# A fused attention and snake-activation kernel: the opening's order of work, and the last output rows in two column parts

## The chip, the cores and the metric

The kernel runs on one core of a Trainium2 chip. A core has a matrix engine (TensorE, PE in the profile, with its weight loads listed apart as PEld), VectorE (DVE), ScalarE (ACT), GpSimd (POOL) and SyncE (SP), which only issues DMAs here. POOL and ACT issue DMAs too. Each engine takes its own instructions strictly in the order in which the program gives them; semaphores tie the engines together, so an instruction that waits holds up all that stands behind it on its engine.

The metric is the device time of one execution in microseconds, lower is better. Three runs of the kernel before gave 377.85, 378.79 and 378.56 us, so the median is 378.56 us.

## The reference, cut to what matters

```python
# q, k, v: (8, 8, 576, 64); bias_table: (32, 8); w_in: (512, 2048); w_out: (2048, 512); alpha: (2048,)
scores = q @ k.T / sqrt(64) + bias_table[bucket(|i - j|)]     # per batch and head
attn   = softmax(scores)
x      = (attn @ v), heads side by side                         # (4608, 512)
h = x @ w_in
g = h + sin(alpha * h) ** 2 / (alpha + 1e-9)
out = g @ w_out                                                 # (4608, 512) float32
```

The bucket of a distance is the distance itself below 16, grows with its logarithm up to 128 and is the last bucket beyond. So the bias differs from a constant only in a band of about 128 keys on each side of the diagonal.

## The kernel before

**Work.** There are eight batches (index t). A batch has eight heads, taken as four pairs (index p), and 576 queries and keys. `plan_unit` makes one unit of attention: a score product on PE (keys on the partitions, a pair of heads side by side), `exp` on ACT out of PSUM, and, for the blocks that touch the band, a multiplication on DVE with `m2r`, which holds exp(bias) relative to the last bucket, row by row shifted. Unit kinds are A (128 keys by 512 queries, two heads), C (the last 64 keys; its band part is `mhr`, multiplied on POOL for pairs 1 to 3 of batch 0 and on DVE otherwise), B and X (the last 64 queries). `plan_av` multiplies the weights with v on PE, divides by the row sum on DVE (`norm_av`, lines 933 to 941), turns the result on PE or by a transposing DMA, and copies it to `xT`. `plan_moe_in` takes 512 rows of x at a time: for each of 16 chunks of `w_in` four matmuls, `Sin` and often `Square` on ACT, the other squares and the combination to `g` on DVE. `plan_mo` makes the output: 16 accumulating matmuls of 512 columns for 128 rows, one copy out of PSUM (`outs`), one DMA of 256 KB from SP. There are nine blocks of 512 output rows; the last block's last rows are the end of the kernel.

**Opening.** Batch 0 does not wait for a staged and transposed copy of q and k. Its pairs are loaded as they are (`nat0` for pair 0 from SP, `nat1` for pairs 1 to 3 from POOL by `load_pair`) and turned on PE (`plan_tr`): k first, then q, each turn copied out of PSUM on DVE to `kT` and `qT`. The small last key block goes to `kt` on POOL (`tail`, line 577). Pair 0 is first cast to 16 bits: k on DVE, q half on ACT (line 514) and half on POOL (line 515).

The band needs a chain of its own: `less_last` times the table on PE (line 509), `exp` on ACT (line 511), a product with a one-hot matrix on PE (line 591), a copy to `e_sb` on ACT (line 594), a DMA of 40 KB to `e_dram` issued by ACT (line 595), and then loads from `e_dram` issued by SP: `m2r` for heads 0 and 1, `mhr` in two DMAs, `m2r` for heads 2 and 3 and for heads 4 to 7 (lines 599 to 602). Behind those SP issues four loads of v for heads 4 to 7 (`load_v32`), which land in the memory of `w_out` and are cast on POOL (`cast_v`).

POOL's queue carries `load_pair`, the loads of v for the last keys (`load_vt`) and for heads 2 and 3 (`load_vh`), the casts of v, the key tails, the C multiplications, the clearing of batch 1's buffers (`clear`), `w_in` in four DMAs (`load_w_in16`, two calls of two), batch 1's q and k and `w_out` (`loads2`) and batch 1's v (`loads3`). Batch 1's q and k are turned on PE as well (`plan_tr` with t = 1), in the middle of the first block's `Sin` work.

PE would otherwise stand idle in the opening; filler matmuls on zeros (`warm`, `warm1`, and `pad` behind some tasks) fill part of it.

**What sets the order.** Apart from a short fixed start (lines 482 to 515), the order on every engine is worked out by a list planner when the program is built (`Plan.run`). Each task has an estimated duration per engine, dependences, a priority (`pri`, lower first) and an earliest time in the planner's own clock (`nb`). The planner always emits the task that can start first, and among those within 0.02 us of each other the one with the lower priority. The constants `T_...` (lines 218 to 241) are such earliest times: for the turns of pair 0 (`T_FIRST`) and of pairs 1 to 3 (`T_PAIR`), the second table product (`T_E`), the v loads and casts (`T_V0`, `T_VA`, `T_VB`), the band multiplications of pairs 0 to 3 (`T_M2`) and of the C units (`T_MH`), `clear` (`T_CL`), `w_in` (`T_WI`), `alpha` (`T_AL`: time and priority), batch 1's turns (`T_TR1`: k, q) and the quarters of `w_out` (`T_WO`). They are the author's picture of when data arrive; a real wait is by semaphore, whatever the planner thought.

Of the kernel before, what the change touches and what calls it, by code (L numbers as in the profile page):

```python
# [20 lines left out]
def t_pe(n):  # L21
    return n / 2400.0 + 0.0025
# [192 lines left out]
T_START = 4.0  # L215
SPLIT = {0: 3, 1: 3}
PRI_S = 0
T_WI = 16.7
T_E = 5.9
T_CL = 20.5  # L220
T_FIRST = (5.2, 6.3)
T_PAIR = ((7.0, 7.4), (8.8, 9.4), (11.0, 11.6))
T_ACT = ()
T_M2 = (13.0, 14.5, 16.0, 16.0)
T_MH = 15.8
T_RST = 25.0
T_V0 = (7.5, 8.2, 8.9, 9.6)
T_VA = (10.5, 11.0)
T_VB = (16.3, 17.8, 18.3, 18.8)
T_AL = (20.0, 100)  # L230
LATE = 100
T_LD = 33.0
AV_LATE = 9000
# [2 lines left out]
NORM0 = 1200  # L236
SQ = {"ACT": 0.52, "DVE": 0.38}
T_V = ((15.5, 19.0), (50.0, 50.0))
T_TR1 = (36.5, 38.0)
T_W = (25.5, 30.5)  # L240
T_WO = (41.0, 43.5, 46.5, 49.5)
WARM0 = 8
WARM1 = 5
WARM_LAG = 0.3
WARM_GAP = 0.12
WARM_FROM = 7.3
# [19 lines left out]
def kernel(  # L266
# [239 lines left out]
    warm(WARM0)  # L506
    for _ in range(WARM1):
        warm1(7, 192)
    full(pb[0:NB, 1, 0:H], less_last, tabN, True, True)
    warm1(7, 192)  # L510
    nc.scalar.activation(out=tabE, in_=pb[0:NB, 1, 0:H], func=AF.Exp)
    cast0(0, nc.vector)
    x0 = nat0[:, 1].rearrange("s two (i d) -> s i two d", i=SI)
    nc.scalar.activation(out=natb[:, 1, :, 0], in_=x0[:, :, 0], func=AF.Copy)
    P_.tensor_copy(out=natb[:, 1, :, 1], in_=x0[:, :, 1])

    def loads2():
# [22 lines left out]
    def plan_tr(t, p, kq, pri, nb, deps=()):  # L540

        b, c = Buf("mo"), Cell()

        def mm(e):
            c.v = bank(b).bitcast(F16)
            for i in range(SI):
                x = i * SN
                if t == 0 and p == 0:
                    nc.tensor.transpose(
                        out=c.v[:, x : x + SN], in_=natb[:, kq, i], identity=id_sb[0:SN, 0:SN]  # L550
                    )
                    continue
                for z in range(2):
                    h = 2 * p - 2 + z if t == 0 else 2 * p + z
                    nc.tensor.transpose(  # L555
                        out=c.v[64 * z : 64 * z + 64, x : x + SN],
                        in_=(nat1 if t == 0 else nat2)[:, kq, h, D * i : D * i + D],
                        identity=id_sb[0:SN, 0:SN],
                    )

        def cp(e):
            pin = c.v[:, 0:S].rearrange("d (i p) -> d p i", i=SI)

            dst = (kTs, qTs)[kq][t][:, p, :]
            copy_on(e, dst.rearrange("d (p i) -> d p i", i=SI), pin)

        m = plan.add({"PE": 0.4 if t == 0 and p == 0 else 0.5}, mm, deps, pri, nb, new=[b])
        if t == 0:
            m.pad = (256,) if p else (192,) * (5 if kq else 1)
        eng = {"DVE": 0.75, "ACT": 0.6}  # L570
        if t == 0:
# [12 lines left out]
        return [x], [plan.add({"POOL": 0.4 if t == 0 else 0.5}, tail, [x], pri + 30)]  # L584

    def plan_table():

        b = Buf("h")

        def mm(e):  # L590
            full(bank(b)[0:H, 0:EW], tabE, phi_sb, True, True)

        def cp(e):
            nc.scalar.activation(out=e_sb, in_=bank(b)[0:H, 0:EW], func=AF.Copy)  # L594
            nc.scalar.dma_start(
                out=e_dram.ap()[:, 0:H].rearrange("r h x -> h r x"),
                in_=e_sb.unsqueeze(1).to_broadcast([H, NE, EW]),
            )
            load_m2r(nc.sync, 0, 2, 0)
            load_mhr(nc.sync)  # L600
            load_m2r(nc.sync, 2, 4, 3)
            load_m2r(nc.sync, 4, H, 4)
            for h in range(4, H):
                load_v32(h)

        x = plan.add({"PE": 0.25}, mm, [], -1100, nb=T_E, new=[b])
        plan.add({"ACT": 1.0}, cp, [x], -1100, use=[b])

    def plan_v0():
        plan.add({"POOL": 1.4}, lambda e: load_pair(3), [], -950, nb=5.8)  # L610
        for i in range(2):
            plan.add({"POOL": 0.45}, lambda e, i=i: cast_v(i), [], 9004 + i, nb=T_VA[i])
# [12 lines left out]

# [317 lines left out]
    def plan_av(t, parts, u, ub, done, base, dma):  # L943
# [154 lines left out]

    def plan_mo(b, a):

        mb, ob, m = Buf("mo"), Buf("outs"), Cell()
        for f in range(NF):

            def mm(e, f=f):
                if f == 0:
                    m.v = bank(mb)
                full(
                    m.v, gcell[b].v[:, f, 128 * a : 128 * a + 128], w_out16[:, f, :],
                    f == 0, f == NF - 1,
                )  # L1110

            mo_last[:] = [plan.add({"PE": t_pe(512)}, mm, mo_last[:] + [gdone[(b, f)]],
                                   500000000 + 4 * b + a, nb=T_WO[f // 4] if b == 0 else 0.0, new=[mb] if f == 0 else [],
                                   use=[gbuf[b]] if f == 0 else [gbuf[b], mb])]
            mo_last[0].fill = True

        def cp(e):
            o = new_outs()
            copy_on(e, o, m.v)
            r0 = 512 * b + 128 * a  # L1120
            nc.sync.dma_start(out=out[r0 : r0 + 128, :], in_=o)

        y = plan.add({"DVE": t_dve(512), "ACT": t_act(512)}, cp, mo_last[:], CP_PRI,
                     new=[ob], use=[mb])
        y.s_only = True

    def set_table(name):
        nc.scalar.preload_act_table_set(name)  # L1128
# [83 lines left out]
```

## Time and profile before

| | us |
|---|---|
| median of 3 runs | 378.56 |
| the profiled execution | 378.73 |
| its span, from the first to the last instruction | 377.0 |
| PE busy | 367.7 |
| ACT busy | 311.8 |
| DVE busy | 260.7 |
| POOL busy | 91.7 |
| mean granted TensorE clock | 0.998 |

The time of an execution has 1.73 us beside the span of its instructions. The page of the profile lists busy times, the span in 40 slices, the DMA queues, the chain of work that ended last, and groups of instructions. The timeline view lists instructions in order of time: start, duration, engine, line and what is written from what, the number of instructions merged in the row, and in brackets how long the engine stood idle before it and who released it. The chain view lists start, duration and what. The view of DMA issues has the number of issues, the size of one and the median time from issue to landing. The view by windows has the busy time of each engine in a stretch.

### The profile page before, as it was taken

How to read it: one execution, taken by the hardware profiler on the slowest of the kernel's cores; microseconds unless marked ns; L12 is line 12 of the kernel's file. 1: busy time of each engine (PE TensorE's matmuls, PEld its weight loads, DVE VectorE, ACT ScalarE, POOL GpSimd, SP SyncE). 2: the span in 40 equal slices, each digit the busy share in tenths (PEclk: the TensorE clock that was granted, in tenths of full speed). 3: DMA queues.
4: the chain of work that ended last, by engine and by line, in shares of the span. 5: the costliest groups of instructions: out<-in, count | busy, mean ns of one | idle time of the engine just before them, and what ended most of it. 6: DMA issues, size and time to landing. Idle time of an engine off the chain costs nothing.

```text
span 377.0 us, 8905 instructions
## 1 busy us (share of the span) xinstructions
PE 367.7 (98%) x3568; PEld 195.7 (52%) x3568; DVE 260.7 (69%) x563; ACT 311.8 (83%) x426; POOL 91.7 (24%) x132
## 2 busy tenths in 40 slices
PE   8889899999999999999999999999999999999995
PEld 4464445644464446864554455445675465444442
DVE  4596867688678867695769676976788677939000
ACT  2988999999898899897979797979897997969111
POOL 7476370064001900091007300550032000000000
PEclk9999999999999999999999999999999999999999
DMA  9989999399627992499349962999299220010212
GB/s 172 149 159 207 200 170 154 71 142 124 101 57 163 85 156 79 84 114 161 87 84 145 141 105 54 148 137 132 57 142 84 62 70 16 0 56 3 83 57 84
DMA packets 148970, 40.49 MB, mean 107 GB/s; under 512 B 137064, under 2 KB 143296, under 8 KB 148928
## 3 DMA queue, kind: packets, MB, share of 16 engines
q0 software_dynamic: 96032, 17.67, 57.9%
q1 hardware_dynamic: 52720, 22.16, 25.1%
q8 instruction: 28, 0.46, 0.5%
q10 hardware_dynamic: 176, 0.09, 0.1%
q14 instruction: 14, 0.11, 0.1%
HBM read 37.73 MB, written 16.56 MB: 144 GB/s over the span
## 4 chain that ended last, share of the span: by engine, by line
PE 87%; DMA 6%; ACT 3%; POOL 2%; SPq 1%; issue 0%; DVE 0%; ACTq 0%
PE pb L453 86%; DMA nat<-in_q_dram 3%; ACT u L692 3%; DMA w_out<-in_v_dram 1%; DMA e_dram<-e_sb 1%; POOL w_in L434 1%; PE pb L555 1%; POOL v L418 0%; SPq L469 0%; PE pb L1009 0%; SPq L476 0%; POOL u L709 0%; POOL nat L428 0%; ACT outs L536 0%; ACT e_sb L594 0%
## 5 line engine op out<-in xcount | busy, mean ns | idle before, releaser
L692 ACT ACTIVATE u<-pb 128x1024 f16<-128x1024 f32 (+1 forms) x146 | 136.0, 1020 | 15.7 <-PE pb L453 15.3
L453 PE MATMUL pb<-w_out,g 128*128 128x512 f16 x576 | 138.3, 380 | 0.0
L453 PE MATMUL pb<-xT,w_in 128*128 128x512 f16 (+4 forms) x704 | 127.9, 340 | 0.0
L1067 DVE SCALAR_TENSOR_TENSOR g<-sq,inv_a,pb 128x512 f16<-128x512 f16 x144 | 101.1, 743 | 10.4 <-PE pb L453 5.6
L1053 ACT ACTIVATE s<-pb,alphaT 128x512 f16<-128x512 f32 x144 | 92.8, 691 | 13.2 <-PE pb L453 12.3
L453 PEld LDWEIGHTS <-w_in 128*128 128x128 f16 x704 | 64.4, 98 | 57.3 <-DMA w_in<-in_moe_w_in_dram 0.4
L453 PEld LDWEIGHTS <-g 128*128 128x128 f16 x576 | 52.6, 98 | 63.4 <-issue 8.5
L723 DVE TENSOR_TENSOR u<-u,m2r 128x512 f16<-128x512 f16 (+1 forms) x128 | 61.9, 494 | 27.5 <-ACT u L692 24.4
L453 PEld LDWEIGHTS <-u 128*128 128x128 f16 x1152 | 44.4, 97 | 9.4 <-issue 2.8
L398 POOL COPY kt<-kT 64x256 f16<-64x256 f16 x12 | 5.1, 427 | 173.4 <-DMA kT<-staged_k 173.1
L453 PE MATMUL pb<-qT,kT 64*128 64x64 f16 (+1 forms) x512 | 44.3, 286 | 0.5 <-ACT u L692 0.2
L453 PE MATMUL pb<-v,u 128*128 128x65 f16 x1024 | 44.5, 193 | 0.2 <-ACT u L692 0.2
L1060 ACT ACTIVATE sq<-s 128x512 f16<-128x512 f16 x66 | 41.5, 637 | 1.2 <-DVE g L1067 0.3
L1062 DVE TENSOR_TENSOR sq<-s 128x512 f16<-128x512 f16 x78 | 32.6, 426 | 14.0 <-ACT s L1053 12.9
L938 DVE TENSOR_TENSOR xn<-pb,rd 128x256 f16<-128x256 f32 (+2 forms) x59 | 28.5, 483 | 2.0
L453 PE MATMUL pb<-vh,u 128*128 128x130 f16 x128 | 28.2, 220 | 0.3 <-DVE xn L938 0.2
L453 PEld LDWEIGHTS <-kT 64*128 64x128 f16 x512 | 16.1, 94 | 23.7 <-issue 16.1
L403 POOL DMA_DIRECT2D v<-in_v_dram x28 | 24.7, 896 | 6.1 <-DMA nat<-in_k_dram 2.3
L536 ACT ACTIVATE outs<-pb 128x512 f32<-128x512 f32 x10 | 6.0, 597 | 23.2 <-PE pb L453 23.2
L937 DVE RECIPROCAL rd<-pb 128x4 f32<-128x4 f32 (+2 forms) x59 | 11.0, 187 | 16.0 <-PE pb L453 15.1
L538 DVE COPY outs<-pb 128x512 f32<-128x512 f32 x26 | 17.9, 687 | 3.6 <-PE pb L453 3.6
L1128 ACT ACT_TABLE_LOAD x15 | 19.2, 1283 | 0.3
(74 smaller groups left out, 188.1 us busy)
## 6 DMA issues: line engine op xcount, KB each, us to landing
out_dram<-outs SPq DMA_DIRECT2D x36, 256.0 KB, 2.3
v<-in_v_dram POOLq DMA_DIRECT2D x28, 128.0 KB, 4.8
staged_k<-in_k_dram POOLq DMA_DIRECT2D x6, 576.0 KB, 8.6
staged_q<-in_q_dram POOLq DMA_DIRECT2D x6, 576.0 KB, 13.0
w_in<-in_moe_w_in_dram POOLq DMA_DIRECT2D x4, 512.0 KB, 8.4
w_out<-in_moe_w_out_dram POOLq DMA_DIRECT2D x4, 512.0 KB, 16.7
w_out<-in_v_dram SPq DMA_DIRECT2D x6, 128.0 KB, 5.4
xT<-xn SPq DMA_TRANSPOSE x47, 2.4
```

Of the source, the lines that this page charges most:

```text
L403: nc.gpsimd.dma_start(out=vs[t % 2][:, c, :, 0:D], in_=vp[128 * c : 128 * c + 128],)
L453: nc.tensor.matmul(out=out, lhsT=lhsT, rhs=rhs, start=start, stop=stop)
L538: k_of(e).tensor_copy(out=o, in_=i)
L692: nc.scalar.activation(out=o, in_=x, func=AF.Exp, scale=0.125)
L723: nc.vector.tensor_tensor(out=io, in0=io, in1=m2[:, 2 * p : 2 * p + 2, x0 : x0 + hi - lo], op=ALU.mult)
L937: nc.vector.reciprocal(out=r, in_=x[:, :, :, D])
L938: nc.vector.tensor_tensor(out=xn[:, 0:n].rearrange("p c (z d) -> p c z d", z=2), in0=x[:, :, :, 0:D], in1=r.unsqueeze(3).to_broadcast([128 ...
L1053: nc.scalar.activation(out=s16.v, in_=h.v, func=AF.Sin, scale=alphaT[:, f : f + 1])
L1060: nc.scalar.activation(out=sq.v, in_=s16.v, func=AF.Square)
L1062: k_of(e).tensor_tensor(out=sq.v, in0=s16.v, in1=s16.v, op=ALU.mult)
L1067: nc.vector.scalar_tensor_tensor(out=gcell[b].v[:, f, :], in0=sq.v, scalar=inv_a[:, f : f + 1], in1=h.v, op0=ALU.mult, op1=ALU.add,)
L1128: nc.scalar.preload_act_table_set(name)
```

## The change

Six things change, nearly all of them places in the order.

1. *Start.* Two filler matmuls of 192 columns instead of five come before the first turn. The first table product leaves the fixed start and becomes a planned task behind the k turn of pair 0, as do its `exp` and the second product, which come before the q turn. The half cast of q that ACT did goes to DVE.
2. *Turns of batch 0.* All of them get other earliest times: pair 0's earlier (4.75 and 5.95 instead of 5.2 and 6.3), those of pairs 1 to 3 later by 0.5 to 1.1.
3. *POOL's loads.* The loads of pair 3's q and k come behind the two `load_vt`.
4. *w_in.* All four DMAs of `w_in` go out at one place, behind a copy of one element of `m2r` (heads 4 to 7) to `tick`, so POOL waits there for the last band rows; the casts of v for heads 4 to 7 come behind them; `clear` is planned later (24.5 instead of 20.5).
5. *alpha* is turned and inverted at planner time 10 instead of 20; the C multiplications may start earlier; batch 1's k turns may come 0.5 earlier and its q turns 1.0 later; the quarters of `w_out` are expected 0.5 to 1.2 earlier; the planner's estimate of batch 0's division shrinks by 0.11 us.
6. *End.* The last 128 output rows are made in two column parts, 384 and 128 columns, each with its own 16 matmuls, copy and DMA.

```diff
-T_WI = 16.7
-T_E = 5.9
-T_CL = 20.5
-T_FIRST = (5.2, 6.3)
-T_PAIR = ((7.0, 7.4), (8.8, 9.4), (11.0, 11.6))
+T_WI = 16.8
+T_TAB = 5.2
+T_CL = 24.5
+T_FIRST = (4.75, 5.95)
+T_PAIR = ((7.9, 8.5), (9.3, 10.2), (11.6, 12.3))
-T_M2 = (13.0, 14.5, 16.0, 16.0)
-T_MH = 15.8
+T_M2 = (13.0, 14.8, 16.0, 16.0)
+T_MH = 14.2
-T_V0 = (7.5, 8.2, 8.9, 9.6)
+T_V0 = (5.8, 6.4, 8.9, 9.6)
+T_P3 = 7.0
-T_VB = (16.3, 17.8, 18.3, 18.8)
-T_AL = (20.0, 100)
+T_VB = (19.5, 19.5, 19.5, 19.5)
+T_AL = (10.0, 560)
-T_TR1 = (36.5, 38.0)
+T_TR1 = (36.0, 39.0)
-T_WO = (41.0, 43.5, 46.5, 49.5)
+T_WO = (40.5, 43.0, 45.7, 48.3)
-WARM1 = 5
+WARM1 = 2
...
-    full(pb[0:NB, 1, 0:H], less_last, tabN, True, True)
-    warm1(7, 192)
-    nc.scalar.activation(out=tabE, in_=pb[0:NB, 1, 0:H], func=AF.Exp)
     cast0(0, nc.vector)
-    nc.scalar.activation(out=natb[:, 1, :, 0], in_=x0[:, :, 0], func=AF.Copy)
+    nc.vector.tensor_copy(out=natb[:, 1, :, 0], in_=x0[:, :, 0])
...
-            m.pad = (256,) if p else (192,) * (5 if kq else 1)
+            m.pad = (256,) if p else (192,) * (2, 3)[kq]
...
+        x = plan.add({"PE": 0.06}, less, [], -1200, nb=T_TAB, new=[a])
+        x.pad = (256,)
+        x = plan.add({"ACT": 0.12}, ex, [x], -1200, use=[a])
...
-        x = plan.add({"PE": 0.25}, mm, [], -1100, nb=T_E, new=[b])
-        plan.add({"ACT": 1.0}, cp, [x], -1100, use=[b])
+        x = plan.add({"PE": 0.25}, mm, [x], -1100, new=[b])
+        plan.add({"ACT": 1.1}, cp, [x], -1100, use=[b])
...
-        plan.add({"POOL": 1.4}, lambda e: load_pair(3), [], -950, nb=5.8)
+        plan.add({"POOL": 1.4}, lambda e: load_pair(3), [], 9001, nb=T_P3)
...
-        x = plan.add({"POOL": 1.4}, lambda e: load_w_in16(0, (0, 2)), [], 9020, nb=T_WI, after=vdone[0:1])
-        for hf, nb in ((1, T_WI + 1.5),):
-            x = plan.add({"POOL": 1.4}, lambda e: load_w_in16(1, (0, 2)), [], 9021, nb=nb, after=[x] + vdone)
+        def w_in(e):
+            P_.tensor_copy(out=tick, in_=m2r[0:1, 4, 0:1])
+            for hf in range(2):
+                load_w_in16(hf, (0, 2))
+
+        x = plan.add({"POOL": 2.9}, w_in, [], 8990, nb=T_WI)
...
-        x = plan.add({"DVE": 0.4 + 128 * nq / 960.0}, norm, prev, base + (NORM_PRI if t else NORM0),
+        x = plan.add({"DVE": (0.4 if t else 0.29) + 128 * nq / 960.0}, norm, prev, base + (NORM_PRI if t else NORM0),
...
+        for c0, c1 in ((0, 384), (384, DM)) if (b, a) == (T, 3) else ((0, DM),):
+            mb, ob, m = Buf("mo"), Buf("outs"), Cell()
+            n = c1 - c0
...
+                    full(
+                        m.v[:, 0 : c1 - c0], gcell[b].v[:, f, 128 * a : 128 * a + 128],
+                        w_out16[:, f, c0:c1], f == 0, f == NF - 1,
+                    )
...
+                copy_on(e, o, m.v[:, 0 : c1 - c0])
+                r0 = 512 * b + 128 * a
+                nc.sync.dma_start(out=out[r0 : r0 + 128, c0:c1], in_=o)
```

More of the change, by code (lines that the diff above doesn't have):

```diff
@@ L586, in plan_table, with less, ex @@
     def plan_table():
-        b = Buf("h")
+        a, b = Buf("h"), Buf("h")
+        def less(e):
+            full(bank(a)[0:NB, 0:H], less_last, tabN, True, True)
+        def ex(e):
+            nc.scalar.activation(out=tabE, in_=bank(a)[0:NB, 0:H], func=AF.Exp)
+        x = plan.add({"PE": 0.06}, less, [], -1200, nb=T_TAB, new=[a])
+        x.pad = (256,)
+        x = plan.add({"ACT": 0.12}, ex, [x], -1200, use=[a])
         def mm(e):
@@ L1099, in plan_mo, with mm, cp @@
     def plan_mo(b, a):
[L1101 to L1125, printed above, removed]
+        for c0, c1 in ((0, 384), (384, DM)) if (b, a) == (T, 3) else ((0, DM),):
+            mb, ob, m = Buf("mo"), Buf("outs"), Cell()
+            n = c1 - c0
+            for f in range(NF):
+                def mm(e, f=f, m=m, mb=mb, c0=c0, c1=c1):
+                    if f == 0:
+                        m.v = bank(mb)
+                    full(
+                        m.v[:, 0 : c1 - c0], gcell[b].v[:, f, 128 * a : 128 * a + 128],
+                        w_out16[:, f, c0:c1], f == 0, f == NF - 1,
+                    )
+                mo_last[:] = [plan.add({"PE": t_pe(n)}, mm, mo_last[:] + [gdone[(b, f)]],
+                                       500000000 + 4 * b + a, nb=T_WO[f // 4] if b == 0 else 0.0,
+                                       new=[mb] if f == 0 else [],
+                                       use=[gbuf[b]] if f == 0 else [gbuf[b], mb])]
+                mo_last[0].fill = True
+            def cp(e, m=m, c0=c0, c1=c1):
+                o = new_outs()[:, 0 : c1 - c0]
+                copy_on(e, o, m.v[:, 0 : c1 - c0])
+                r0 = 512 * b + 128 * a
+                nc.sync.dma_start(out=out[r0 : r0 + 128, c0:c1], in_=o)
+            y = plan.add({"DVE": t_dve(n), "ACT": t_act(n)}, cp, mo_last[:], CP_PRI,
+                         new=[ob], use=[mb])
+            y.s_only = True
     def set_table(name):
```

## The prediction

> **What bounds the kernel now.** I read the page's busy times first, then the windows, the chain of work that ended last, and then the timeline of the first 57 us engine by engine.
>
> ```profile
> PE 367.7 (98%) x3568; PEld 195.7 (52%) x3568; DVE 260.7 (69%) x563; ACT 311.8 (83%) x426; POOL 91.7 (24%) x132
> ```
>
> ```profile
> 57.00:373.20 316.20, 315.91 (x2974) 168.22 (x2972) 220.55 (x470) 264.93 (x358) 57.10 (x64) 1.00 0.78 95
> ```
>
> From 57 us to the last matmul PE (the first busy figure, behind the length of the stretch) misses 0.29 us of 316.2. That part can only be moved, not shortened, unless the order in it gets worse. So the change is worth what it takes off the opening and off the last copy and DMA.
>
> ```profile
> 7.77 4.72 DMA e_dram<-e_sb
> ...
> 28.87 12.23 DMA nat<-in_q_dram
> ```
>
> ```profile
> out_dram<-outs SPq DMA_DIRECT2D x3, 256.0 KB, 2.0
> ```
>
> The chain (start, duration) names two transfers of the opening, the table's way to DRAM and batch 1's q, which lands at 41.1. Each is slow beside the DMA issues of the kernel's end, where 256 KB land in 2.0 with no neighbours. ACT's rows show what the opening is made of:
>
> ```profile
> 9.29 10.44 ACT L692 ACTIVATE u<-pb 128x1024 f16<-128x1024 f32 x12 [1.54 <-PE pb L453]
> 20.25 1.02 ACT L692 ACTIVATE u<-pb 128x1024 f16<-128x1024 f32 x1 [0.52 <-PE pb L453]
> 21.31 0.38 ACT L536 ACTIVATE xT<-pb 128x256 f16<-128x256 f16 x1
> ...
> 28.37 1.28 ACT L1128 ACT_TABLE_LOAD   x1
> ...
> 32.22 1.84 ACT L1053 ACTIVATE s<-pb,alphaT 128x512 f16<-128x512 f32 x3 [0.48 <-PE pb L453]
> ...
> 41.63 0.65 ACT L536 ACTIVATE qT<-pb 128x576 f16<-128x576 f16 x1 [0.90 <-PE pb L555]
> ```
>
> The first exp starts at 9.29. Then ACT works through 20 exps until 28.37, its longest hole 0.52; 3.85 us later the first Sin starts, and in the Sin stretch ACT has one hole of 0.90, for batch 1's q. So ACT sets the pace here, and four spans follow each other: start, exps, change-over, Sin.
>
> **The change part by part.** The sum is made against the profiled execution, 378.73 us (span 377.0 and 1.73 around it), 0.17 above the median of 378.56.
>
> *Start (fewer fillers, k turn before the table, q's half cast on DVE).*
>
> ```profile
> 4.66 0.63 PEld L453 LDWEIGHTS <-zz 128*128 128x128 f16 x4 [0.28 <-issue]
> ```
>
> ```profile
> 5.59 0.27 PE L453 MATMUL pb<-tabN,phi_sb 32*32 32x8 f32 x2
> 5.79 0.34 PE L453 MATMUL pb<-zz 128*128 128x192 f16 x1
> 5.93 0.69 PE L549 MATMUL pb<-id_sb,natx 96*128 96x96 f16 x6
> 6.41 0.36 PE L453 MATMUL pb<-zz 128*128 128x192 f16 x1
> 6.71 0.41 PE L453 MATMUL pb<-phi_sb,tabE 32*8 32x512 f16 x1
> 7.05 0.43 PE L549 MATMUL pb<-id_sb,natx 96*128 96x96 f16 x6
> 7.32 0.58 PE L453 MATMUL pb<-zz 128*128 128x192 f16 x5
> 7.99 0.45 PE L555 MATMUL pb<-id_sb,nat 96*64 96x96 f16 x12
> 8.37 0.53 PE L453 MATMUL pb<-zz 128*128 128x256 f16 x4
> 8.83 0.39 PE L453 MATMUL pb<-qT,kT 64*128 64x512 f16 x2
> ```
>
> ```profile
> 5.90 0.17 ACT L511 ACTIVATE tabE<-pb 32x8 f16<-32x8 f32 x1 [2.38 <-PE pb L453]
> ```
>
> ```profile
> 7.52 0.76 DVE L538 COPY qT<-pb 128x576 f16<-128x576 f16 x1
> ```
>
> Four small fillers take 0.63 us, so three fewer save 0.48 and the k turn starts at 5.11 instead of 5.93. It holds PE 0.48 us (5.93 to 6.41), two pads 0.32, so the first table product starts at 5.91; its exp comes 0.31 behind its start and takes 0.17, to 6.39; the second product follows at about 6.5 instead of 6.71, and the q turn, now right behind it, 0.34 later at 6.84 instead of 7.05. Its copy starts 0.47 behind it and takes 0.76, to 8.07. Before, the copy was ready at 8.28 but the score product waited until 8.83 behind pair 1's k turn (7.99) and four pads; that turn is now planned behind it. So the score product starts at about 8.17 and the first exp, 0.46 later, at 8.63: 0.66 sooner. I take 0.6, with ends of 0.2 (only the order of 0.21 us on PE counts) and 0.8. Moving the half cast costs nothing: DVE has nothing else before the k turn's copy, and the q turn that needs it comes at 6.8. Later turns of pairs 1 to 3 are hidden as long as ACT has exps (10.44/12 = 0.87 us each) to work on; PE needs 0.39 for a score product and 0.45 for a turn.
>
> *Exps: the band rows, alpha, C parts.*
>
> ```profile
> 15.81 0.42 DVE L723 TENSOR_TENSOR u<-u,m2r 128x512 f16<-128x512 f16 x1 [2.19 <-DMA m2r<-e_dram]
> ```
>
> ```profile
> 24.23 0.16 DVE L634 COPY alphaT<-pb 128x16 f32<-128x16 f32 x1
> ```
>
> ```profile
> 20.00:28.00 8.00, 6.93 (x116) 4.95 (x114) 7.76 (x26) 7.28 (x11) 6.72 (x17) 1.00 0.79 141
> ```
>
> DVE (third busy figure) waits for the first band rows until 15.81 and is then busy 7.76 of 8.00 us between 20 and 28: a second limit behind ACT (fourth figure, 7.28), and the likely source of ACT's holes of 0.72 there, because PE runs weight-times-v products, which need DVE's multiplications, ahead of score products. The change takes alpha's three small instructions (0.16 for the first, so about 0.6 with the gaps) out of this stretch, to a place where DVE only copies turns, and the table's chain starts 0.2 sooner. Pair 3's loads going out behind the small v loads may free the way for the table's 4.72 us; I cannot see the share, so the bounds for its landing are 0 and 2.7 sooner (down to the quiet 2.0). I take 0.3 of a possible 0.72 off ACT's holes; the other end is +0.5, a hole more because a turn or the alpha product holds PE's queue.
>
> *Change-over.*
>
> ```profile
> 29.63 0.93 PE L453 MATMUL pb<-xT,w_in 128*128 128x512 f16 x3
> ...
> 365.69 7.50 PE L453 MATMUL pb<-w_out,g 128*128 128x512 f16 x34
> ```
>
> Three `w_in` matmuls of the change-over take 0.93 from 29.63, the last one's length included, against 3 · 0.22 at the pace of the kernel's end (7.50 us for 34, in the second row); so PE loses at most 0.3 to the late `w_in`, and I count none of it; if `w_in` had stayed where it is, an opening 0.9 sooner would wait for it, so the earlier issue is needed rather than worth something. The last turn stands behind two groups of three `w_in` matmuls; the division planned 0.11 shorter may let it pass the second group (0.65). I take 0.2, ends 0 and 0.6.
>
> *POOL: w_in, casts, clear, batch 1's loads.*
>
> ```profile
> m2r<-e_dram SPq DMA_DIRECT2D x1, 384.0 KB, 5.4
> ```
>
> ```profile
> 21.35 1.45 POOL L434 DMA_DIRECT2D w_in<-in_moe_w_in_dram  x2
> 22.80 1.10 POOL L418 CAST v<-w_out 128x256 f16<-128x256 f32 x3
> 23.83 1.40 POOL L434 DMA_DIRECT2D w_in<-in_moe_w_in_dram  x2
> 25.25 0.45 POOL L709 TENSOR_TENSOR u<-u,mhr 128x128 f16<-128x128 f16 x1
> ...
> 28.04 0.83 POOL L428 DMA_DIRECT2D nat<-in_k_dram  x1
> ```
>
> ```profile
> 24.88 0.22 PE L453 MATMUL pb<-vh,u 128*128 128x130 f16 x1
> ```
>
> The first band load, issued some 0.2 behind the table's landing at 12.49, arrives for DVE at 15.81; the last is the third of its kind and takes 5.4, so it lands near 20.4; with the chain 0.3 to 0.5 sooner POOL leaves its wait at about 20.0. The four issues take 1.45 + 1.40, to 22.9. Behind them wait the casts of v (two for pair 2 end at 23.6, two for pair 3 near 24.8 with a C multiplication between) and that multiplication. They are wanted by pair 2's weight-times-v products, the first of which now starts at 24.88, and 0.9 sooner then, at 24.0: covered by 0.4. If the band rows come over 0.4 later than that, this cover is gone and each further microsecond costs one. `clear` (2.5 us by the planner) now falls behind the last C multiplication, and batch 1's k is issued up to 1.5 later than the 28.04 of now. That is hidden: its transfer stands behind all of `w_in` in the queue and took until 41.1 for q. The queue starts 21.35 − 20.1 = 1.25 sooner and stays full, so q lands at about 39.9. The q turn is planned 1.0 later, so PE no longer stops for it and ACT's 0.90 hole goes: I take 0.8; ends 0.9, and −1.5 if q keeps its 12.23 from issue to landing and is issued 1.5 later. Next late is the last quarter of `w_out`, 1.25 sooner in the same queue.
>
> *End.*
>
> ```profile
> 373.27 0.60 ACT L536 ACTIVATE outs<-pb 128x512 f32<-128x512 f32 x1 [2.85 <-PE pb L453]
> ```
>
> A matmul of 512 columns takes 7.50/34 = 0.22 us; in two parts 16 · 0.22 · (3/4 + 1/4) plus a few hundredths for 16 more instructions, +0.08. The last copy shrinks from 0.60 (512 columns) towards the 0.38 of 256 columns and by the same slope to 0.27 for 128: −0.33. The DMA of 64 KB instead of 256 lands after 1.5 to 2.0 instead of 2.0: I take −0.25. The first part's copy and issue lie beside the second part's 0.9 us of matmuls. Together −0.5, ends −0.15 and −0.8.
>
> [...]
>
> Sum: −0.6 − 0.3 − 0.2 − 0.8 − 0.5 = −2.4, so 376.3 on the profiled execution and 376.2 on the median.
>
> **The rivals.**
> *Hidden anyway.* If q of batch 1 lands no sooner (41.1), all that the opening gains turns into a longer hole at its turn, and only the end gains: 378.56 − 0.5 = 378.1. For it: `loads2` goes out later. Against: 10 us of queue ahead of it.
> *Band rows later (slower).* The two v loads that now pass pair 3 on POOL's queue are made of small pieces and run beside the table's 40 KB. If the table lands x later, the saturated DVE stretch, POOL's wait, the casts and `w_in` all move by x; against that stand alpha's 0.6 and the end's 0.5. It decides from x = 1.1, and is slower by 0.3% from 2.2; at 3 it gives 378.56 + 3 − 1.1 = 380.5. For it: 4.72 us for 40 KB shows how much that transfer suffers from its neighbours. Against: pair 3's two loads also leave its neighbourhood.
> *Half of it.* DVE, not ACT, holds the exps, so the first exp's gain is lost and alpha's is not, and the hole of q closes half: 378.56 − 1.3 = 377.3.
> *All of it.* Every term at its good end: −0.8 − 0.72 − 0.6 − 0.9 − 0.8 = −3.8, 374.8; I take 375.0, since `w_in` and `w_out` come only 1.25 sooner.
> [...]
>
> **How the numbers follow.** This kernel's runs differ by 0.25%, so 0.3% (1.1 us) is about what can be told from no change. Chances: the forecast 0.42, half of it 0.16, all of it 0.08, so faster 0.66; hidden 0.12 and half clock 0.06, so same 0.18; band rows later 0.16, slower. The forecast's own range is 375.4 to 377.2. To leave out no more than 2 in 10 the range goes from 375.0 (all of it) past 378.1 (hidden) and the lower part of the slower case, to 379.2.
>
> **What would show it.** First exp near 8.6; first band multiplication at or before 15.6; POOL's wait for `m2r` ending near 20; the exps' end near 27.5 and the first Sin near 31.1; no stop at the first q turn of batch 1 near 40; two last copies and a span that ends about 2.9 instead of 3.1 us (377.0 − 373.87) behind the end of the last copy. I am wrong if `e_dram` lands after 13.5, if ACT's holes between exps add up to over 1.5 us, if the q turn waits again, or if PE shows idle time beyond 0.5 us after 57.

## The result and the profile after

Over 20 runs each on one chip the changed kernel takes 375.62 us (median; 374.46 to 379.48) and the kernel before 378.51 (377.52 to 379.37). The ratio is 0.9942 with a 95% interval of 0.9919 to 0.9965: faster by 0.6%, between the forecast of 376.2 and the low end of 375.0.

The profiled execution took 376.99 us (span 375.1, mean granted clock 0.991), 1.4 above the median. Its busy times, on the page:

```profile
PE 367.5 (98%) x3576; PEld 196.4 (52%) x3576; DVE 262.3 (70%) x569; ACT 309.7 (83%) x421; POOL 92.7 (25%) x133
```

ACT's timeline of the opening (start, duration) is to be laid beside the rows shown of before (first exp 9.29, table load 28.37, first `Sin` 32.22). The table load marks the end of the exps:

```profile
8.45 1.02 ACT L704 ACTIVATE u<-pb 128x1024 f16<-128x1024 f32 x1 [1.57 <-PE pb L454]
10.26 1.02 ACT L704 ACTIVATE u<-pb 128x1024 f16<-128x1024 f32 x1 [0.79 <-PE pb L454]
12.07 1.02 ACT L704 ACTIVATE u<-pb 128x1024 f16<-128x1024 f32 x1 [0.79 <-PE pb L454]
13.77 0.60 ACT L704 ACTIVATE u<-pb 128x512 f16<-128x512 f32 x1 [0.67 <-PE pb L454]
14.74 11.19 ACT L704 ACTIVATE u<-pb 128x1024 f16<-128x1024 f32 x13 [0.38 <-PE pb L454]
...
28.55 1.28 ACT L1143 ACT_TABLE_LOAD   x1
...
32.91 1.27 ACT L1065 ACTIVATE s<-pb,alphaT 128x512 f16<-128x512 f32 x2 [0.48 <-PE pb L454]
```

The first exp is 0.84 sooner, yet the first `Sin` is 0.69 later: four holes between the exps that follow (0.79, 0.79, 0.67 and 0.38, together 2.63) eat the gain. The windows (length, PE's busy time and count, and, third from the end, the granted clock) say why:

```profile
6.00:8.00 2.00, 1.02 (x12) 0.64 (x11) 1.64 (x3) 0.59 (x1) 1.94 (x5) 1.00 1.28 201
8.00:9.00 1.00, 1.00 (x13) 0.45 (x14) 0.00 (x0) 0.56 (x1) 1.00 (x3) 0.53 1.31 177
9.00:14.00 5.00, 5.00 (x47) 2.35 (x43) 2.27 (x3) 2.75 (x4) 3.34 (x8) 0.50 1.21 147
14.00:15.00 1.00, 1.00 (x5) 0.18 (x5) 0.60 (x3) 0.62 (x2) 0.32 (x2) 0.55 0.99 215
15.00:17.00 2.00, 2.00 (x45) 1.30 (x43) 1.25 (x3) 2.00 (x3) 0.00 (x0) 1.00 0.90 233
```

PE runs at half clock from about 8.1 to 14.9 (granted 0.53, 0.50 and 0.55 in the windows from 8 to 15, and 1.00 ahead of them and behind). So this execution shows the half clock, to which the forecast gave a chance of 0.06, and the changed kernel without it needs another trace (`again`, below). And still it ends sooner than before. One reason is that PE, idle for 1.42 of the 17 us between 40 and 57 in the kernel before, does not stop there at all (a stop is a time in which PE waits).

### The profile page after: what moved, and what is told of

Its sections match the earlier page's. It is cut to its first block, busy times and chain, and to the rows that moved or that the text cites. A ratio compares the mean times of both kernels' runs of the same rounds, so it can differ in the third digit from the quotient of the medians.

```text
span 375.1 us, 8928 instructions
## 1 busy us (share of the span) xinstructions
PE 367.5 (98%) x3576; PEld 196.4 (52%) x3576; DVE 262.3 (70%) x569; ACT 309.7 (83%) x421; POOL 92.7 (25%) x133
## 3 DMA queue, kind: packets, MB, share of 16 engines
q1 hardware_dynamic: 52864, 22.16, 24.2%
## 4 chain that ended last, share of the span: by engine, by line
PE 93%; ACT 4%; DMA 1%; DVE 0%; issue 0%; POOL 0%; SPq 0%; ACTq 0%
PE pb L454 91%; ACT u L704 4%; PE pb L553 1%; DMA natx<-in_q_dram 1%; PE pb L1021 1%; DVE qT L536 0%; POOL natx L513 0%; PE pb L547 0%; DVE xn L950 0%; DVE u L735 0%; SPq L429 0%; ACT outs L534 0%; ACT xT L534 0%; PE pb L643 0%; PE pb L931 0%
## 5 line engine op out<-in xcount | busy, mean ns | idle before, releaser
L454 PE MATMUL pb<-w_out,g 128*128 128x512 f16 (+2 forms) x592 | 138.6, 374 | 0.0
L454 PEld LDWEIGHTS <-g 128*128 128x128 f16 x592 | 53.5, 98 | 63.0 <-issue 9.1
L454 PE MATMUL pb<-qT,kT 64*128 64x64 f16 (+1 forms) x512 | 45.1, 289 | 1.9 <-ACT u L704 1.0
L454 PE MATMUL pb<-v,u 128*128 128x65 f16 x1024 | 43.7, 193 | 0.0
L1072 ACT ACTIVATE sq<-s 128x512 f16<-128x512 f16 x65 | 41.1, 640 | 1.2 <-DVE g L1079 0.3
L534 ACT ACTIVATE outs<-pb 128x512 f32<-128x512 f32 (+2 forms) x11 | 6.2, 568 | 19.9 <-PE pb L454 19.9
## 6 DMA issues: line engine op xcount, KB each, us to landing
w_out<-in_moe_w_out_dram POOLq DMA_DIRECT2D x4, 512.0 KB, 14.9
```

Source lines behind the costliest of these rows:

```text
L454: nc.tensor.matmul(out=out, lhsT=lhsT, rhs=rhs, start=start, stop=stop)
L1072: nc.scalar.activation(out=sq.v, in_=s16.v, func=AF.Square)
```

## Experiments

One table first, from each kernel's trace: the first exp, DVE's first band multiplication, the first `Sin`, what PE is busy of the 17 us from 40 to 57, and the end of the last copy. The median and the ratio are those of the timed runs. *Half clock* marks the two traces in which the granted clock fell. Each trace is of one execution.

| kernel | first exp | first band | first Sin | PE 40–57 | last copy ends | median | ratio (95%) |
|---|---|---|---|---|---|---|---|
| before | 9.29 | 15.81 | 32.22 | 15.58 | 373.87 | 378.51 | |
| changed (half clock) | 8.45 | 16.17 | 32.91 | 17.00 | 372.16 | 375.62 | 0.9942 (0.9919–0.9965) |
| `again` | 7.95 | 15.01 | 31.41 | 17.00 | 370.81 | 375.37 | 0.991 (0.9897–0.9923) |
| `fill_hole` | 8.78 | 14.60 | 31.00 | 17.00 | 370.25 | 376.67 | 0.9942 (0.9929–0.9954) |
| `start_only` | 8.11 | 15.20 | 32.34 | 16.70 | 372.28 | 377.95 | 0.9976 (0.9959–0.9993) |
| `tail_only` | 9.28 | 15.52 | 32.04 | 15.72 | 373.61 | 378.69 | 0.9997 (0.9988–1.0005) |
| `no_tail` | 8.40 | 14.90 | 31.30 | 17.00 | 370.83 | 375.54 | 0.992 (0.9906–0.9933) |
| `undo_win` | 8.13 | 14.61 | 31.41 | 17.00 | 370.66 | 375.84 | 0.9928 (0.9916–0.9941) |
| `undo_start` | 8.91 | 15.87 | 31.58 | 15.71 | 372.79 | 377.57 | 0.9972 (0.9962–0.9983) |
| `undo_turns` | 8.11 | 15.15 | 31.55 | 15.84 | 372.38 | 377.17 | 0.9967 (0.9956–0.9979) |
| `start_turns` | 7.99 | 14.77 | 31.22 | 15.81 | 372.08 | 377.16 | 0.9957 (0.9937–0.9976) |
| `turns_only` | 9.21 | 15.16 | 31.82 | 16.30 | 372.99 | 377.79 | 0.9977 (0.9967–0.9986) |
| `undo_wo` (half clock) | 8.18 | 15.55 | 32.02 | 16.51 | 372.43 | 375.83 | 0.9936 (0.9918–0.9954) |
| `more_warm` | 9.05 | 15.24 | 31.64 | 17.00 | 370.89 | 376.05 | 0.9942 (0.9921–0.9963) |

### The changed kernel again, and with its first hole filled

`again` has no edit. `fill_hole` adds six filler matmuls of 384 columns to the changed kernel, four behind pair 0's q turn and two behind the second table product:

```diff
+            m.more = (384,) * 4 if kq and not p else ()
...
+        x.more = (384,) * 2
```

> The changed kernel once more, unaltered. In its profiled execution the granted clock fell to 0.5 from 8.1 to 14.9 us; its 20 runs spread from 374.5 to 379.5 where those of before spread from 377.5 to 379.4. Theory A (the gain is the sum of the parts, the half clock a rare disturbance): median near 375.5, an execution whose granted clock stays at 1.00 in the opening starts its first Sin near 31 us instead of 32.9. Theory B (half clock in the opening is usual and accounts for the whole spread): every run over 376 us has a mean clock below 0.997, and the profile shows half clock again. A run over 378 us with a mean clock of 1.00 would be neither, and asks for a third cause.

> The changed kernel with six more filler matmuls of 384 columns, two behind the second table product and four behind pair 0's q turn, where PE stood idle for 0.4 and 0.6 us; the order of everything else is the same. If the holes of PE in the opening let the clock fall (the rival of the prediction), the granted clock stays at 1.00 from 6 to 15 us in every run, runs near 376 to 377 us disappear, and the median falls by 0.2 to 0.5 us to about 375.2. If the holes have nothing to do with it, the clock falls in some runs as before and the median stays or rises by up to 0.1.

`again` kept its clock (0.999) and took 375.27 to 375.63 in four runs, as theory A has it. ACT's timeline:

```profile
7.95 10.89 ACT L704 ACTIVATE u<-pb 128x1024 f16<-128x1024 f32 x12 [1.04 <-PE pb L454]
...
27.05 1.28 ACT L1143 ACT_TABLE_LOAD   x1
...
31.41 1.84 ACT L1065 ACTIVATE s<-pb,alphaT 128x512 f16<-128x512 f32 x3 [0.48 <-PE pb L454]
```

So the half clock cost the profiled execution 1.5 at the first `Sin` (32.91 against 31.41) and 1.4 at the end. In `fill_hole` the clock stayed at 1.00 in the trace and the first 17 exps came without a hole, but the trace is of its fastest run (375.2). The other four took 376.11 to 376.93, three of them at a clock of 1.00, so the median did not fall by 0.2 to 0.5 but rose by 1.0 to 1.3 (376.67 beside 375.62 and 375.37). That the half clock came from the hole is therefore not shown by this pair. What fills the hole also delays the first exp (8.78 against 7.95 in `again`); what made the four runs longer is open.

The windows of before and, below, of `again`, over the stretch that holds batch 1's turns:

```profile
40.00:49.00 9.00, 7.86 (x122) 4.12 (x123) 7.83 (x14) 8.07 (x15) 3.75 (x9) 1.00 1.23 202
49.00:57.00 8.00, 7.72 (x105) 3.50 (x96) 5.02 (x14) 7.70 (x10) 5.18 (x5) 1.00 2.31 160
```

```profile
40.00:49.00 9.00, 9.00 (x137) 4.77 (x136) 8.41 (x16) 8.57 (x14) 5.01 (x12) 1.00 1.33 204
49.00:57.00 8.00, 8.00 (x75) 3.31 (x74) 4.45 (x12) 7.06 (x9) 3.73 (x2) 1.00 2.39 166
```

And PE's products with `w_out` between 9 and 57 us, in the groups by line of before and of `again`:

```profile
L453 PE MATMUL pb<-w_out,g 128*128 128x512 f16 x20 | 5.0, 379 | 0.0
```

```profile
L454 PE MATMUL pb<-w_out,g 128*128 128x512 f16 x31 | 7.8, 379 | 0.0
```

Eleven more of them are done by 57: at the 0.22 us of the kernel's end 2.43 us. That is most of the 2.74 by which the last copy starts sooner (373.27 to 370.53); 0.81 of it stand at the first `Sin`, and 1.42 are stops that are gone.

### The start alone, the start undone, more fillers

`start_only` is the kernel before with part 1 and 2 of the change; `undo_start` is the changed kernel without them. `more_warm` gives the changed kernel its three fillers back:

```diff
-WARM1 = 2
+WARM1 = 5
```

> The kernel before with the start alone: three fewer fillers, the k turn ahead of the table's product, q's half cast on DVE, pair 0's turns sooner and the others later. POOL's queue, w_in, alpha, batch 1's turns and the end are as before. By the prediction's sum: first exp at 8.5 to 8.7 and 0.6 us saved, less what waits for the band rows or for batch 1's q later, so 377.9 to 378.5. If batch 1's q, which does not land sooner here, is the limit (the rival 'hidden anyway'), the hole in the Sin stretch grows from 0.9 to 1.5 and the time is that of before within 0.2.

> The changed kernel with the old start: table's product and its exp ahead of the first turns, five fillers ahead of them, the old pads and planned times of the turns. Forecast's terms: 0.6 for the start (and at most the 0.3 of the exps), so 376.0 to 376.3, ratio 0.993 to 0.994; first exp near 9.3, exps' end 27.7, first Sin about 32.1. If the start is worth what its exps gained in the run with the start alone (1.44), 376.8, ratio 0.9955 and a first Sin at 32.8. If the change-over takes up what the start gives, as it did there (first Sin 32.34 beside 32.22), 375.4 to 375.6, first Sin near 31.4.

> The changed kernel with five fillers of 192 columns ahead of the first turn again instead of two, all else as changed. By the time that the three take, the k turn and the first exp come up to 0.48 later: 375.6 to 375.9, ratio 0.992 to 0.993, first exp at 8.5 to 8.9. If the fillers only use time in which PE would wait for the casts: first exp at 8.0 to 8.4 and 375.4. If the five executions of 20 that took 378.2 to 379.5 come from a start with fewer fillers, none of these runs lies over 377.5.

The start alone gained 0.8 us, and undoing it cost about 2 (377.57 beside 375.62 and 375.37), more than any of the theories had: neither is what the first exp says. `more_warm` moves the first exp by itself. It comes 1.10 later than in `again`, but DVE's first band multiplication only 0.23 later, and the first `Sin` follows by the same 0.23. Its three runs with a clock of 0.999 or 1.00 took 375.34 to 375.77, about as long as those of `again`:

```profile
9.05 14.13 ACT L704 ACTIVATE u<-pb 128x1024 f16<-128x1024 f32 x16 [1.01 <-PE pb L454]
...
31.64 1.84 ACT L1065 ACTIVATE s<-pb,alphaT 128x512 f16<-128x512 f32 x3 [0.48 <-PE pb L454]
```

In the table the first `Sin` stands 16.40 us behind the first band multiplication in `again`, `fill_hole`, `no_tail`, `more_warm` and `undo_turns`, and 16.41 in the kernel before. The chain of `again` (start, duration, what) goes through that multiplication:

```profile
6.94 2.56 DMA e_dram<-e_sb
...
9.58 5.33 DMA m2r<-e_dram
...
15.01 0.43 DVE u L735
15.44 0.56 DVE kT L536
...
19.68 1.88 DVE u L735 x4
...
23.41 1.02 ACT u L704
```

It leads from the table's transfer over the first band load to DVE's work and has no exp before 23.41. The chains of `more_warm`, `undo_turns` and `undo_win` go the same way, that of `no_tail` over a later band load. So in these kernels the arrival of the band rows and DVE's work behind it set the opening, not the first exp. In `fill_hole`, where the exps come without a hole, the chain has exps instead:

```profile
11.04 1.62 ACT u L709 x2
12.66 8.43 ACT u L709 x10
```

The two limits thus lie close together. DVE's and SP's timelines of `again` have the first use of a band row and the issue of its load (before: 15.81, shown in the prediction, and 12.57):

```profile
15.01 0.43 DVE L735 TENSOR_TENSOR u<-u,m2r 128x512 f16<-128x512 f16 x1 [1.83 <-DMA m2r<-e_dram]
```

```profile
9.58 0.37 SPq L470 DMA_DIRECT2D m2r<-e_dram  x1
```

These are single traces, and the band rows vary by themselves. The kernel before, `tail_only` and `turns_only` have the same opening, yet SP issues the first band load at 12.57, 12.14 and 10.78, the first band multiplication comes at 15.81, 15.52 and 15.16, and the first `Sin` at 32.22, 32.04 and 31.82. So the 0.81 at the first `Sin` is known to about 0.4. The traces also show that a sooner issue brings less than it promises. From issue to first use the load took 5.4 us when it was issued at 9.58 (`again`), 3.9 to 5.2 when issued between 10.25 and 11.20, and 3.4 and 3.2 from 12.14 and 12.57.

`undo_start` has its band rows at 15.87 but a shorter way from there (15.71), and its first `Sin` is only 0.17 later than in `again`. Its loss is elsewhere: PE misses 1.29 us of 40 to 57. `start_only` shows the reverse, a first `Sin` that came no sooner (32.34) and a smaller stop (0.30).

### Batch 1's turns and POOL's order

`undo_turns` gives the changed kernel the old planned times of batch 1's turns and of the products with `w_out` (below), `undo_wo` the latter alone. `turns_only` is the kernel before with both new ones, `start_turns` is `start_only` with both:

```diff
-T_TR1 = (36.0, 39.0)
+T_TR1 = (36.5, 38.0)
...
-T_WO = (40.5, 43.0, 45.7, 48.3)
+T_WO = (41.0, 43.5, 46.5, 49.5)
```

`undo_win` gives the changed kernel the old place of `w_in` on POOL, without the wait for the last band rows:

```diff
-        x = plan.add({"POOL": 2.9}, w_in, [], 8990, nb=T_WI)
+        x = plan.add({"POOL": 1.4}, lambda e: load_w_in16(0, (0, 2)), [], 9020, nb=T_WI, after=vdone[0:1])
+        for hf, nb in ((1, T_WI + 1.5),):
+            x = plan.add({"POOL": 1.4}, lambda e: load_w_in16(1, (0, 2)), [], 9021, nb=nb, after=[x] + vdone)
...
+T_CL = 20.5
+T_VB = (16.3, 17.8, 18.3, 18.8)
```

> The changed kernel with POOL's old order: w_in at its old place between the casts of v, the casts and the clear at their old times, no tick. Forecast's terms: without the 0.8 of batch 1's q and the 0.2 of the change-over, about 376.4 (1.0 above 375.4), ratio 0.9945. Theory from the run with the start alone (exps' end 1.44 sooner, first Sin not): the sooner start needs the sooner w_in, so that the change-over grows from 4.4 to over 5 us, the first Sin comes at about 32.3 instead of 31.4 and the time is 377 to 377.9, ratio 0.996 to 0.998. Third: w_in's place matters to nothing, because the late q turns alone close the hole: 375.4, ratio 0.9915, first Sin at 31.4.

> The changed kernel with the old planned times of batch 1's turns (36.5 and 38.0 instead of 36.0 and 39.0) and of the products with w_out (41.0 to 49.5 instead of 40.5 to 48.3). Forecast: q lands at about 39.6, a q turn planned for 38 stops PE's queue until then, and ACT's hole of 0.9 ahead of the first qT copy is back in part (1.3 less the 0.4 of work in between): 375.8 to 376.3, ratio 0.9925 to 0.994. Rival: the sooner w_in alone closes the hole, since in the run with the start alone, with the old times, it was closed too: 375.4, ratio 0.991 to 0.992, the wait of the turn for q under 0.3.

> The changed kernel with the old planned times of the w_out products alone (41.0 to 49.5), batch 1's turns at the new ones. If the turns' times close PE's stop: 375.4, ratio 0.991 to 0.992, PE busy 9.00 of 9.00 between 40 and 49. If the w_out products are what fills it: 376.5 to 377.2, ratio 0.995 to 0.997, and a stop of about 1 us ahead of the first of them, near 47.

> The kernel before with nothing but the new planned times of batch 1's turns (36.0, 39.0) and of the w_out products. If the times alone close PE's stop between 40 and 49 (1.14 in the kernel before): 377.4, ratio 0.997. If the order of that stretch also needs the sooner start, since undoing the start brought a stop of 1.03 back with the new times: 378.5, ratio 0.999 to 1.0, a stop of about 1 us in that stretch. If q is what it waits for (landing at 41.1) it is the turn that stops, else DVE's copy of kT.

> The kernel before with the new start and the new planned times of batch 1's turns and of the w_out products; POOL's work, alpha, pair 3's loads and the tail are as before. If these two parts carry the gain (undoing POOL's part cost 0.3, undoing the start 2.1, the turns' times 1.7), about 375.8, ratio 0.993, PE without a stop between 40 and 49, first Sin near 31.4 to 31.6. If the moved w_in, pair 3's loads or alpha are needed as well: a change-over of over 5 us as in the run with the start alone (first Sin 32.3) and 376.8 to 377.9, ratio 0.9955 to 0.998.

Between the two rows of its chain that the prediction shows, the kernel before has no exp. SP issues the loads of v for heads 4 to 7 behind the band loads, POOL waits for them with its casts, and `w_in` and batch 1's q stand behind those casts:

```profile
15.54 5.41 DMA w_out<-in_v_dram
...
21.01 0.39 POOL v L418
21.41 1.40 POOL w_in L434 x2
```

So with this order on POOL a sooner landing of the table brings q forward too. In `start_only` the first of these loads goes out at 14.71, q is issued at 28.00 instead of 28.87 and lands at 40.3 instead of 41.1. With the old order of the turns its stop for q is 0.23 instead of 1.14. In `turns_only` q lands at 40.4 and its turn stands behind two k turns, at 40.87; PE misses 0.15 between 40 and 49. In `again` q lands at 39.6 and its turn starts at 41.33. So both the sooner q and its later turn close the hole, and `start_only` shows that the sooner q alone does most of it.

`undo_win` stays within 0.5 of the changed kernel, its interval overlaps with those of both sets of runs, and PE has no stop. The new place of `w_in` is thus not needed to close the hole. An earlier `w_in` is not excluded by it: with the sooner opening it goes out at 19.06 and 22.12 here too, instead of 21.35 and 23.83, and q lands at 38.7. The first `Sin` stands 16.80 behind the first band multiplication instead of 16.40. That is no wait for `w_in`, since the change-over is 4.36 as in `again`. DVE's four band multiplications take 0.41 longer than in `again` (19.68, in the chain above), while POOL's casts of v lie beside them (timelines of DVE and POOL, `undo_win`):

```profile
19.27 2.29 DVE L731 TENSOR_TENSOR u<-u,m2r 128x768 f16<-128x768 f16 x4
```

```profile
20.53 1.64 POOL L419 CAST v<-w_out 128x256 f16<-128x256 f32 x3
```

In `again` three such casts took 1.09, from 22.16. That the two slow each other is read from this one pair of traces.

`undo_turns` loses 1.6 to 1.8, more than either theory had. There q is not late (it lands at 38.5, and its turn stands behind two k turns at 41.25), but the last turns stand at 45.63 instead of 44.67, and PE stops until DVE has copied the k turn among them. What waits is a product with `w_out` just ahead of score products with kT; why it needs that copy the profile does not say (PE's timeline):

```profile
45.63 0.70 PE L553 MATMUL pb<-id_sb,nat 96*64 96x96 f16 x24
47.36 0.38 PE L454 MATMUL pb<-w_out,g 128*128 128x512 f16 x1 [1.03 <-DVE kT L536]
```

`undo_start` shows the same stop, as long, at 47.39: with the old start the new planned times lead the planner to the order that `undo_turns` has. With `undo_wo` PE has 9.00 of 9.00 between 40 and 49 and the median is 375.83, so the turns' times matter, and those of the `w_out` products are worth 0.2 to 0.5 at most. In its trace, in which the clock fell, PE stops once for a late quarter of `w_out`, for 0.49 at 50.88.

Moved alone, the times gain 0.7 (`turns_only`), and with the new start 1.4 (`start_turns`, whose runs vary from 375.4 to 381.9). In both the stop does not go but moves on, to the next late transfer. PE's timelines of `start_turns` and `turns_only`:

```profile
50.74 1.24 PE L453 MATMUL pb<-w_out,g 128*128 128x512 f16 x5 [1.19 <-DMA w_out<-in_moe_w_out_dram]
```

```profile
51.21 1.46 PE L453 MATMUL pb<-w_out,g 128*128 128x512 f16 x6 [0.55 <-DMA w_out<-in_moe_w_out_dram]
```

So three stops of 0.5 to 1.2 us lie in wait between 40 and 57 (q, kT, `w_out`). The traces that avoid all three have the new start, the new times of the turns and POOL's part of the change, with or without the moved `w_in`. What POOL's part adds over `start_turns` is seen in the last quarter of `w_out`. It lands at 50.7 to 51.6 in the five kernels with POOL's old part (before, `tail_only`, `start_only`, `start_turns`, `turns_only`) and at 48.8 to 49.8 in those traces that have the new start and POOL's part and kept their clock (`undo_win` among them, 49.3). Which piece of that part does it (pair 3's loads later, alpha, the C parts) was not taken apart further.

### The last rows

`tail_only` is the kernel before with the two column parts (its loop below), `no_tail` the changed kernel without them:

```diff
+        for c0, c1 in ((0, 384), (384, DM)) if (b, a) == (T, 3) else ((0, DM),):
```

> The kernel before with the end alone: the last 128 rows in parts of 384 and 128 columns. [...] No other difference in the trace.

> The changed kernel with the last output rows in one piece again (one copy of 512 columns, one DMA of 256 KB). Forecast's term for the end, 0.5: about 375.9, ratio 0.993 where the whole change had 0.991. Rival, from the run that made the split alone and gained nothing (378.69 against 378.72): the end is worth nothing, 375.4, ratio 0.991 to 0.992. The last copy takes 0.60 in both; by the forecast's term the span ends about 3.1 behind the end of the last copy with a copy that ends 0.26 later, by the rival the span is that of the whole change, 373.8.

`tail_only`: the last copy and the DMA issues at the end.

```profile
373.33 0.28 ACT L536 ACTIVATE outs<-pb 128x128 f32<-128x128 f32 x1 [0.40 <-PE pb L453]
```

```profile
out_dram<-outs SPq DMA_DIRECT2D x1, 64.0 KB, 2.0
```

The copy is 0.28 instead of 0.60 and ends 0.26 sooner, but the span ends 3.49 behind it instead of 3.13, at 377.1 (before 377.0). The ratio of 0.9997 (0.9988 to 1.0005) leaves at most 0.45 us; the timed runs of `no_tail` against the changed kernel (375.54 beside 375.37 and 375.62) show no clear difference either. The other traces speak differently. In the eight others with two parts the same DMA landed in 1.6, as here in `again`:

```profile
out_dram<-outs SPq DMA_DIRECT2D x1, 64.0 KB, 1.6
```

From the start of the last copy to the end of the span these eight took 3.22 to 3.30 us, the five with one piece 3.62 to 3.73 (before 3.73, `no_tail` 3.67), and `tail_only` 3.77. So `tail_only`'s trace is the odd one out, and the two parts may be worth up to about 0.4, which its timed runs neither show nor exclude. What the end is worth is not settled.

## Why the prediction was right, point by point

The time and the sign were right, with a sum of 2.4 against a measured 2.9. The terms were not all right. They are compared here with `again`, whose clock did not fall.

**Start, exps and change-over (0.6 + 0.3 + 0.2).** The first `Sin` came 0.81 sooner, against 1.1. Each piece was missed: the first exp gained 1.34, the exps' end 1.32 (27.05, against a forecast of about 27.5), and the change-over grew by 0.51 (3.85 to 4.36) where I had taken 0.2 off. The failing step is "ACT sets the pace here": as `more_warm` shows, the first exp may come 1.1 later for 0.2 us. The chain that the prediction showed two rows of had hinted at it, since between those rows it has no exp. The rival of the half, in which DVE and not ACT holds the exps and the first exp's gain is lost, had the mechanism; what it missed is that the band rows come sooner too, by 0.80. I had looked for that in the landing of the table, which SP's issue of the first band load follows: 9.58 in `again` instead of 12.57. Only 0.8 of these 3.0 reached DVE, because from its issue to its first use the band load then took 5.4 instead of 3.2 us. Part of both figures is the spread between executions shown above.

**Batch 1's q (0.8).** Right in direction and too small: the stops between 40 and 57 cost 1.42 and are gone. That q would land at about 39.9 and its turn no longer wait came true (39.6 in `again`). The cause was half right: the later turn helps, but q lands sooner without the new place of `w_in` too (38.7 in `undo_win`). POOL left its wait at 18.21, sooner than the 20.0 foreseen (POOL's timeline of `again`; 20.18 in the profiled execution of the changed kernel):

```profile
18.21 0.24 POOL L630 COPY tick<-m2r 1x1 f16<-1x1 f16 x1 [0.69 <-DMA m2r<-e_dram]
18.44 2.90 POOL L435 DMA_DIRECT2D w_in<-in_moe_w_in_dram  x4
```

The medians of `undo_win` price that at 0.2 to 0.5, with intervals that overlap. "Next late is the last quarter of `w_out`" was right: `start_turns` stops there for 1.19. What I did not foresee is that DVE's copy of kT can stop PE about as long as q did (1.03 against 1.14).

**End (0.5).** Not shown. The timed runs of `tail_only` put it at 0 and at most 0.45, the spans of the other traces at up to 0.4. The copy came out as forecast (0.60 to 0.28). The sign at which I would have seen the gain, a span that ends about 2.9 behind the last copy, did show (2.94 and 2.99, against 3.02 to 3.13 with one piece), but the timed runs do not bear it out. The 0.25 for the DMA took a landing in 1.5 to 2.0. No run shows the 1.5: 64 KB landed in 1.6 in `again`, where 256 KB landed in 2.0, and in 2.0 in `tail_only`.

**The sum.** From the kernel before to `again` the span shrinks by 3.2: the last copy starts 2.74 sooner, and from there to the end it takes 3.27 instead of 3.73. Of the 2.74 the first `Sin` has 0.81, the stops 1.42, and PE's idle time after 57 us 0.16 (PE is busy 310.72 and 310.88 of 311). That makes 2.4; the rest is not accounted for. The forecast had 1.1 for the first, 0.8 for the second, nothing for the third, and 0.5 for the end. That its sum came near the measured 2.9 is in part luck: the opening was priced too high, the stops too low, and the two errors partly cancel.

**The rivals.** *Hidden anyway* and *band rows later* did not happen: no stop for q, and the band rows at 15.01. *Half clock*, with a chance of 0.06 and counted as no change, did: in the profiled execution it cost about 1.5 (the first `Sin` at 32.91, against 31.41 in `again`), and with it came one of the signs of being wrong, holes of over 1.5 us between the exps (2.63). It came as a fall, from a granted clock of 1.00 between 6 and 8 us to 0.50 between 9 and 14.

## What carries over

Where a list planner writes the order, the parts of a change do not add: undoing the start cost about 2 us, adding it alone gained 0.8. With another start the planner also orders batch 1's turns 30 us later in another way, and a stop that one order avoids comes back or moves on to the next late transfer. Price such a change by following the chain and PE's stops with what releases each, and look for the next late transfer in the same stretch. And before pricing a sooner first step, check what the last step of the stretch stands at a fixed distance from; here that was mostly the first band multiplication, not the first exp.

## What the hardware did that was not expected

**A fall to half clock without a long idle time.** In two traces PE's clock was halved after 2 us in which PE was busy about half of the time, and no single stop was over 0.85. In the changed kernel PE was busy 1.02 of the 2 us ahead of it, with two stops (PE's timeline):

```profile
6.63 0.43 PE L547 MATMUL pb<-id_sb,natx 96*128 96x96 f16 x6 [0.38 <-POOL natx L513]
...
7.91 0.50 PE L454 MATMUL pb<-qT,kT 64*128 64x512 f16 x2 [0.60 <-DVE qT L536]
```

The second trace is `undo_wo`; a row of its timeline and its windows:

```profile
16.70 0.27 PE L454 MATMUL pb<-zz 128*128 128x256 f16 x1 [0.85 <-DVE kT L536]
```

```profile
15.00:17.00 2.00, 1.05 (x7) 0.35 (x6) 1.45 (x3) 2.00 (x3) 0.24 (x2) 1.00 1.11 290
17.00:18.00 1.00, 0.83 (x9) 0.45 (x8) 1.00 (x3) 1.00 (x3) 0.91 (x2) 0.79 1.13 230
18.00:20.00 2.00, 2.00 (x34) 1.90 (x32) 1.97 (x7) 1.07 (x2) 1.33 (x4) 0.50 0.63 121
20.00:21.00 1.00, 1.00 (x7) 0.23 (x4) 1.00 (x3) 0.28 (x1) 1.00 (x2) 0.51 0.27 12
21.00:22.00 1.00, 1.00 (x19) 0.66 (x18) 1.00 (x3) 1.00 (x2) 1.00 (x3) 1.00 0.83 141
```

At half clock PE spent 0.42 + 2 + 0.98 = 3.4 us here (a window's loss of clock, doubled), and 0.94 + 5 + 0.90 = 6.8 in the changed kernel. That the stops caused the fall is an inference from two traces. `again` with nearly the same order (1.40 busy of the same 2 us) did not fall, and neither did the kernel before after a stretch with less work than either:

```profile
15.00:17.00 2.00, 0.84 (x9) 0.30 (x5) 1.19 (x3) 2.00 (x4) 0.04 (x1) 1.00 0.80 173
```

Nor does it seem to take the hole from 6 to 8. `more_warm` has none in its trace (PE is busy 2.00 of 2 from 6 to 8), and three of its six runs still have a mean clock of 0.994 or 0.995, as low as in the 3.4 us of half clock of `undo_wo` (0.995).

The price depends on the kernel. Executions with a mean granted clock of 0.995 or less took 375.9 to 377.0 in the changed kernel (others 375.5 in the median), 376.3 to 377.8 in `more_warm` (others 375.3 to 375.8), but 378.0 to 378.9 in the kernel before, which is its usual time.

**When PE becomes fast varies by itself.** The six turns of pair 0's k, all issued at 4.9 to 5.0 with the same start, took 0.43 us in `again` and 0.69 in `no_tail` and `fill_hole`. It is not seen in the granted clock, which reads 1.00 in both, and no cost of it is seen (first `Sin` 31.41, 31.30 and 31.00).

**Open.** Five of the first 20 executions of the changed kernel took 378.2 to 379.5 us with a mean granted clock of 0.998 to 1.00, one of `undo_wo` 379.7, and one each of `start_only` and `start_turns` 382.0 and 381.9 (another of `start_only` 380.1, with a clock of 0.991); 82 of the kernel before never took more than 379.4. They widen the interval of the result. No trace caught one. `more_warm` was to tell whether the fewer fillers cause it; its two longest runs (377.70, 377.78) had the clock at 0.995 and are of the other kind, so it tells nothing.
